# A packed-attention mixer on one core: w1's last quarter, a written plan for batch 0, and the turning of p

## The chip, the core and the metric

The kernel runs on one core of a Trainium2 chip. The metric is the device time of one execution in microseconds. The core's engines are PE (TensorE; its weight loads are shown as PEld), DVE (VectorE), ACT (ScalarE), POOL (GpSimd) and SP (SyncE, which here issues nearly all DMAs). Each engine works through its own list of instructions in order, and waits at an instruction until what it needs is there.

## What is computed

Eight batches, eight heads, 576 tokens, head dimension 64, 32 packing queries per head. Cut to what matters:

```python
def sm_attn(qq, kk, vv):
    s = scale * np.matmul(qq, kk.transpose(0, 1, 3, 2))
    a = np.exp(s - np.max(s, axis=-1, keepdims=True))
    a = a / (np.sum(a, axis=-1, keepdims=True) + 1e-09)
    return np.matmul(a, vv)
p_packed = sm_attn(p, k, v)                  # 32 packed tokens per head
x = sm_attn(q, p_packed, p_packed)           # back to 576 tokens; heads side by side: 512 columns
h = x.transpose(0, 2, 1) @ U @ V             # mixing over tokens, rank 32
u = x + h.transpose(0, 2, 1)
out = u + np.maximum(u @ w_ch1, 0.0) @ w_ch2 # 512 -> 2048 -> 512
```

[...]

## The kernel before

**Products in three parts.** The large products split each operand into a rounded part and a rest (names ending in h and l), and `mm3` (lines 85 to 89) issues three products for one.

**Conversion.** `float32_of` (line 73) makes a 128 x 512 block of 32-bit floats from its bits: one ACT operation (line 79, or line 150 in `test_w1`) and three on DVE (lines 80 to 82). w1 has 16 such blocks, called chunks here, number n holding row block x and column quarter c; chunks 12 to 15 are the last quarter. w2 has 16 row blocks of 128 rows. A w2 row block is also split into w2h and w2l (`split_w2`, line 163): a cast on ACT and a subtraction, on POOL for block 0 and on DVE for the others. Bits land in the tiles `bits` (2 buffers, for the whole kernel) and `bits2` (2 buffers, first stage only). `load_w1` and `load_w2` put the DMAs on SP.

**First stage (lines 513 to 577).** The packing attention runs in 16 units, two per batch (four heads each). For a unit, `a_turn` turns k with PE transposes and copies it out of PSUM as kT, `a_scores` forms scores s_ps from kT and pT, `a_softmax` takes the maximum on DVE (sm) and the exponential on ACT (e), `a_turn_back` transposes it, `a_pack` multiplies by v, `a_heads` turns the result into ppT. Once per batch `a_p` makes pT: it turns p and sets the heads of the second group in swapped pairs. The loop `for i in range(NU)` emits one unit per turn; `turns[i]` says how many w1 chunks are converted in that turn, and the steps of batch 0's own attention (`first`, from `attention(0)`) go three to a turn from turn 4 on. Turn 13 emits `fold(0, 0)`, turn 14 starts w2. In this stage the order of each engine's list isn't the order in which the code stands: a scheduler that estimates times sets it.

**Main stage (from line 579, `manual_schedule`).** Here the engines' lists are in the order of the code. For every batch b and each of 16 steps kt, `gemm1(kt)` computes 128 rows of the hidden layer into h_ps (two banks, tags h0 and h1), which ACT and DVE evict as hh and hl; `gemm2(kt - 1)` multiplies them with the w2 blocks into four accumulators o. `fold(b, c)` multiplies ppT with a quarter of w1 into t_ps and evicts it as wth and wtl, four steps ahead of its use, so `fold(0, 3)`, at kt = 10 of batch 0, is the first to read w1's last quarter. `add_u` adds u at kt = 6. Beside these stand the side steps: the steps of the next batch's attention (`steps`), in batch 0 also the last four pieces of the packing (`rest`) and w2's conversions and splits. Before, an attention step comes after `gemm1` and one at the end of each kt, padded with empty ones; a piece of `rest` or a step is put between the two halves of `gemm2`; a split and a conversion stand at the end of each kt.

Of the kernel before, what the change touches and what calls it, by code (L numbers as in the profile page):

```python
# [20 lines left out]
def packed_attention_mixer_kernel(  # L21
# [27 lines left out]
    nc = tc.nc  # L49
    B, H, S, D = q.shape  # L50
# [4 lines left out]
    P = 128  # L55
# [3 lines left out]
    NK = DF // P  # L59
# [3 lines left out]
    scale = 1.0 / float(D) ** 0.5  # L63
# [7 lines left out]
    U, V, w1, w2 = (a.bitcast(I32) for a in (U, V, w1, w2))  # L71

    def float32_of(x, t, raw, out=None, tested=False):


        low, high = raw[:, :, 0], raw[:, :, 1]
        out = x if out is None else out.bitcast(I32)
        if not tested:
            nc.scalar.activation(t, high.bitcast(F32), AF.Abs, scale=REBIAS)
        nc.vector.tensor_single_scalar(x, t.bitcast(I32), 3, op=ALU.logical_shift_left)  # L80
        nc.vector.scalar_tensor_tensor(x, high, SIGN, x, op0=ALU.bitwise_and, op1=ALU.bitwise_or)  # L81
        nc.vector.scalar_tensor_tensor(out, low, 29, x, op0=ALU.logical_shift_right, op1=ALU.bitwise_or)
        return out.bitcast(F32)
# [7 lines left out]
    const = ctx.enter_context(tc.tile_pool(name="const", bufs=1))  # L91
# [37 lines left out]
    def w2_parts(kt):  # L129
        return tuple(t[:, kt % 4] for t in w2t[kt // 4])  # L130

    def conv_tile(dtype):
        return pipe.tile([P, DM], dtype, name="os", bufs=4)

    def bits_tile():
        return pipe.tile([P, 512, 2], I32, name="bits", bufs=2)

    chunks = [(x, c) for c in range(NPC) for x in range(4)]
# [9 lines left out]
    def test_w1(n):  # L148
        tests[n] = conv_tile(F32)
        nc.scalar.activation(tests[n], bits["w1", n][:, :, 1].bitcast(F32), AF.Abs, scale=REBIAS)  # L150

    def convert_w1(n):
        x, c = chunks[n]
        float32_of(conv_tile(I32), tests.pop(n), bits.pop(("w1", n)), w1t[x][:, QW * c:QW * c + QW], tested=True)

    def load_w2(kt):
        b = bits["w2", kt] = bits_tile()
        nc.sync.dma_start(out=b.rearrange("p x t -> p (x t)"), in_=w2[kt * P:(kt + 1) * P, :])

    def convert_w2(kt):  # L160
        return kt, float32_of(conv_tile(I32), conv_tile(F32), bits.pop(("w2", kt)))

    def split_w2(kt, x):
        hi, lo = w2_parts(kt)
        nc.scalar.copy(hi, x)
        (nc.gpsimd if kt == 0 else nc.vector).tensor_tensor(lo, x, hi.bitcast(F32), op=ALU.subtract)

# [232 lines left out]
    sA = actx.enter_context(tc.tile_pool(name="sA", bufs=2, reuse_waits="tile"))  # L400
# [4 lines left out]
    pn, pT, pps, sums = {}, {}, {}, {}  # L405
# [23 lines left out]
    def a_p(b):  # L429
        t_ps = bank()  # L430
        pT[b] = sA.tile([P, 2, P], F32, name="pT")
        pd = sA.tile([P, 2, 2, D], F32, name="pd", bufs=1)
        nc.gpsimd.tensor_copy(pd, pn[b].unsqueeze(2).to_broadcast([P, 2, 2, D]))
        for i in range(2):
            nc.tensor.transpose(t_ps[:, P * i:P * i + P], pd[:, i].rearrange("p z d -> p (z d)"), ident)
        nc.scalar.activation(pT[b][:, 0], t_ps[:, :P], AF.Copy, scale=scale)
        dst, src = (a.rearrange("p (y z n) -> p z y n", y=2, z=2) for a in (pT[b][:, 1], t_ps[:, P:2 * P]))
        for z in range(2):
            nc.scalar.activation(dst[:, z], src[:, 1 - z], AF.Copy, scale=scale)

    def a_turn(u):
        b, g = UN[u]
# [77 lines left out]
    first = attention(0, res)  # L520
    test_w1(0)

    def some_w1(n):
        convert_w1(n)
        if n + 1 < 16:
            test_w1(n + 1)
        if n + 4 < 16:
            load_w1(n + 4)


    turns = [0, 0] + [1] * 10 + [2, 1, 2, 1]
    n_w1 = 0
    for i in range(NU):
        if i > 0:
            a_turn_back(i - 1, bank_a("m"))
        a_scores(i)
        if i + 1 < NU:
            a_load_v(i + 1)
            a_turn(i + 1)
# [12 lines left out]
        if i >= 4:  # L552
            for _ in range(3):
                if first:
                    first.pop(0)()
        if i == 2:
            uv = load_uv()
        if i == 3:
            prepare_uv(*uv)
        if i == 13:  # L560
            fold(0, 0)
        if i == 14:
            load_w2(0)
            load_w2(1)
            steps = attention(1, res)
            steps.pop(0)()
            split_w2(*convert_w2(0))
            load_w2(2)
# [134 lines left out]
    w2x = None  # L703

    pieces = {3: 2, 8: 0}
    n_w2 = 1

    for n in (20, 19, 18, 15, 15, 14, 13, 12, 12, 11, 5, 0, 0, 0, 0):
        steps.insert(n, lambda: None)
    last, parts = None, []  # L710
    for b in range(B):
        cur = Batch(b)
        oj = None
        ahead = attention(b + 2, res) if b + 2 < B else []
        for kt in range(NK):
            cur.gemm1(kt)
            if b == 0 and kt < 2:
                w2x = convert_w2(n_w2)
                n_w2 += 1
            if oj and kt == 1:  # L720
                store_joint(b - 1, oj)
            if steps and (b < 2 or kt % 4 != 2) and (b, kt) != (1, 0):
                steps.pop(0)()
            if (b, kt) == (0, 5):
                w2_tiles(ctx.enter_context(tc.tile_pool(name="sC", bufs=1, side="right", reuse_waits="tile")), 2)
            if kt > 0:
                cur.gemm2(kt - 1, (rest or steps).pop(0) if b == 0 and (rest or steps) else None)
            elif last:
                last.gemm2(NK - 1)
                last.store()  # L730
                if last.b % 2 == 1:
                    oj = joint(last.b, parts)
            if kt % 4 == 2 and (b, kt) != (B - 1, NK - 2):
                n = b * NPC + kt // 4 + 1
                fold(n // NPC, n % NPC)
            if kt == 6:
                cur.add_u()
            for _ in range(pieces.get(kt, 1)):
                if w2x:
                    split_w2(*w2x)  # L740
                    w2x = None
                    if n_w2 + 1 < NK:
                        load_w2(n_w2 + 1)
                    if 0 < kt and n_w2 < NK:
                        w2x = convert_w2(n_w2)
                        n_w2 += 1
            if steps and kt % 4 != 2 and (b, kt) != (1, 0):
# [45 lines left out]
```

## Time and profile before

| what | us |
|---|---|
| median of 3 runs | 831.68 |
| lowest and highest run | 831.53, 833.7 |
| the profiled execution | 831.53 |
| its span in the profile | 829.7 |
| PE busy in the span | 798.7 |
| DVE, ACT, POOL busy | 351.2, 318.7, 80.1 |

The busy time is a sum over instructions; the overlap of pipelined products is taken out. A row of a timeline has the start in microseconds, the duration, the engine, the line and operation, what it writes and reads, and how many records are grouped; in brackets stands how long the engine had been idle, and what ended that. A row by windows gives, for each stretch, the busy time and number of records of each engine, the clock that PE was granted as a share of the full one, the mean busy share of the DMA engines and their rate in GB/s. A row of waits names the waiting instruction, the instruction it waited for, the sum, the count and the longest. The chain of waits is followed back from the last instruction; its row by line gives the share of the stretch that each line has on it.

### The profile page before, as it was taken

To read this page: it belongs to the slowest core of one execution; us is meant where nothing else is said; L and a number is where in the kernel's file an instruction comes from. 1 tells how busy PE (TensorE), PEld (TensorE's weight loads), DVE (VectorE), ACT (ScalarE), POOL (GpSimd) and SP (SyncE) were. 2 spreads that over 40 slices of the span, in tenths; PEclk is the share of its full clock that TensorE was granted. 3 is DMA by queue.
4 is the path that set the end of the run, shared out by engine and by line. 5 is a ranking of instruction groups with operands and counts; after the bars stand their busy time and mean duration, and the time that the engine had idled before them with its cause. 6 is when DMAs were issued, how large, how long until landed. Compare 5 with 4: busy or idle time off the path is not lost.

```text
span 829.7 us, 15436 instructions
## 1 busy us (share of the span) xinstructions
PE 798.7 (96%) x6224; PEld 643.7 (78%) x6224; DVE 351.2 (42%) x781; ACT 318.7 (38%) x974; POOL 80.1 (10%) x115
## 2 busy tenths in 40 slices
PE   7879698999999999999999999999999999999997
PEld 5556377888788888888888888888888888887886
DVE  3777467773343323433433234333434234332232
ACT  5788664354333332333333232343234232332231
POOL 0222201100111001010011001010101011100000
PEclk8999899999999999999999999999999999999999
DMA  9999764216001220023002120122002200030001
GB/s 299 347 360 358 252 139 127 78 51 188 1 1 47 100 55 2 1 96 92 1 1 89 58 55 2 46 87 57 2 18 90 73 22 1 14 111 1 2 0 64
DMA packets 60310, 70.23 MB, mean 85 GB/s; under 512 B 22864, under 2 KB 41296, under 8 KB 60240
## 3 DMA queue, kind: packets, MB, share of 16 engines
q1 hardware_dynamic: 59920, 68.73, 26.5%
q8 instruction: 49, 0.80, 0.4%
q10 hardware_dynamic: 320, 0.52, 0.2%
q14 instruction: 21, 0.17, 0.1%
HBM read 53.64 MB, written 15.60 MB: 83 GB/s over the span
## 4 chain that ended last, share of the span: by engine, by line
PE 89%; DVE 4%; DMA 3%; ACT 2%; issue 1%; POOL 0%; SPq 0%; ACTq 0%; POOLq 0%
PE o L87 16%; PE o L89 16%; PE o L88 16%; PE h_ps L87 9%; PE h_ps L89 8%; PE h_ps L88 8%; PE t_ps L384 4%; DMA bits<-in_moe_w_ch_dram 2%; PE o L654 2%; PE t_ps L229 2%; DMA vt<-in_v_dram 1%; PE t_ps L327 1%; PE t_ps L249 1%; PE t_ps L255 1%; DVE os L81 1%
## 5 line engine op out<-in xcount | busy, mean ns | idle before, releaser
L87 PE MATMUL o<-w2h,hh 128*128 128x512 f32 x512 | 206.6, 404 | 0.0
L89 PE MATMUL o<-w2h,hl 128*128 128x512 f32 x512 | 202.4, 395 | 0.0
L88 PE MATMUL o<-w2l,hh 128*128 128x512 f32 x512 | 201.9, 394 | 0.0
L637 DVE SCALAR_TENSOR_TENSOR hl<-h_ps,hh 128x256 fp32r<-128x256 f32 x256 | 105.4, 423 | 204.0 <-ACT hj L636 189.9
L634 ACT ACTIVATE hh<-h_ps 128x256 fp32r<-128x256 f32 x256 | 98.6, 386 | 182.9 <-PE h_ps L89 182.5
L87 PE MATMUL h_ps<-ah,wth 128*128 128x320 f32 (+1 forms) x512 | 157.7, 308 | 0.4 <-DVE hl L637 0.3
L88 PE MATMUL h_ps<-al,wth 128*128 128x320 f32 (+1 forms) x512 | 151.6, 296 | 0.0
L89 PE MATMUL h_ps<-ah,wtl 128*128 128x320 f32 (+1 forms) x512 | 151.5, 296 | 0.0
L87 PEld LDWEIGHTS h_ps<-ah,wth 128*128 128x128 f32 x512 | 96.7, 189 | 25.6 <-issue 21.0
L89 PEld LDWEIGHTS o<-w2h,hl 128*128 128x128 f32 x512 | 96.4, 188 | 22.5
L87 PEld LDWEIGHTS o<-w2h,hh 128*128 128x128 f32 x512 | 97.0, 189 | 21.0 <-issue 4.6
L88 PEld LDWEIGHTS o<-w2l,hh 128*128 128x128 f32 x512 | 97.0, 189 | 16.6
L88 PEld LDWEIGHTS h_ps<-al,wth 128*128 128x128 f32 x512 | 96.9, 189 | 1.9
L89 PEld LDWEIGHTS h_ps<-ah,wtl 128*128 128x128 f32 x512 | 97.0, 189 | 0.0
L391 DVE TENSOR_TENSOR wtl<-t_ps,wth 128x256 fp32r<-128x256 f32 x128 | 48.5, 420 | 102.4 <-ACT wth L390 99.0
L390 ACT CAST wth<-t_ps 128x256 fp32r<-128x256 f32 x128 | 43.3, 374 | 110.0 <-PE t_ps L384 102.3
L347 POOL TENSOR_TENSOR al<-aT,ah 128x320 fp32r<-128x320 f32 (+1 forms) x32 | 25.7, 806 | 211.5 <-ACT ah L346 211.5
L290 POOL TENSOR_TENSOR e<-e,m 128x576 f32<-128x576 f32 x16 | 18.6, 1160 | 261.8 <-DVE m L289 261.8
L236 ACT COPY xT<-t_ps 128x256 f32<-128x256 f32 x64 | 21.5, 395 | 38.9 <-PE t_ps L229 38.2
L384 PE MATMUL t_ps<-w1t,ppT 64*32 64x512 f32 x512 | 35.9, 615 | 0.0
L346 ACT CAST ah<-aT 128x320 fp32r<-128x320 f32 (+1 forms) x32 | 13.8, 435 | 43.8 <-DVE aT L345 43.8
L636 ACT ACTIVATE hj<-h_ps 128x64 f32<-128x64 f32 x128 | 28.3, 221 | 0.0
(121 smaller groups left out, 822.3 us busy)
## 6 DMA issues: line engine op xcount, KB each, us to landing
bits<-in_moe_w_ch_dram SPq DMA_DIRECT2D x32, 512.0 KB, 6.4
kx<-in_k_dram SPq DMA_DIRECT2D x16, 576.0 KB, 7.0
x<-in_q_dram SPq DMA_DIRECT2D x16, 576.0 KB, 5.0
vt<-in_v_dram SPq DMA_DIRECT2D x32, 256.0 KB, 6.9
out_dram<-bits SPq DMA_DIRECT2D x32, 256.0 KB, 2.4
aD<-aT SPq DMA_DIRECT2D x16, 288.0 KB, 2.1
aP<-aD SPq DMA_DIRECT2D x32, 128.0 KB, 3.4
ppP<-ppD SPq DMA_DIRECT2D x32, 64.0 KB, 3.1
```

The lines of the kernel that those rows point to most:

```text
L87: nc.tensor.matmul(ps, lhsT=lh, rhs=rh, start=start, stop=False)
L88: nc.tensor.matmul(ps, lhsT=lh, rhs=rl, start=False, stop=False)
L89: nc.tensor.matmul(ps, lhsT=ll, rhs=rh, start=False, stop=stop)
L236: nc.scalar.copy(dst, src[:, a])
L290: nc.gpsimd.tensor_tensor(e, e, m.unsqueeze(2).to_broadcast([P, S // 32, 32]), op=ALU.subtract)
L347: nc.gpsimd.tensor_tensor(al[:, g, ns], aT[:, ns], ah[:, g, ns].bitcast(F32), op=ALU.subtract)
L384: nc.tensor.matmul(f_ps[g][xs], lhsT=ppT[b][zs, g, xs], rhs=w1t[h // 2][zs, QW * c:QW * c + QW], start=True, stop=True)
L390: nc.scalar.copy(hi[:, g], f_ps[g][:, cs])
L391: nc.vector.tensor_tensor(lo[:, g], f_ps[g][:, cs], hi[:, g].bitcast(F32), op=ALU.subtract)
L634: nc.scalar.activation(hh[:, ms], src, AF.Relu)
L636: nc.scalar.activation(hj[:, jslot(self.b, kt), self.js], h_ps[:, LAST], AF.Relu)
L637: nc.vector.scalar_tensor_tensor(hl[:, ms], src, 0.0, hh[:, ms].bitcast(F32), op0=ALU.max, op1=ALU.subtract)
```

## The change

Three things are done. w1's chunks 12 to 15 are no longer converted in the first stage but among batch 0's products, with loads taken in one list (`order`) with w2's. What stands beside batch 0's products is written in a table `plan`: for each kt three places (after `gemm1`, between the halves of `gemm2`, at the end), and letters for a conversion of w2 (c), a split (s), a late w1 chunk (w), an attention step (a) and a piece of `rest` (u). The two tables `turns` and `early` set how many w1 chunks and attention steps each turn of the first stage has. And p is turned without a copy on POOL: four products of p with the identity, or with an identity whose columns are swapped in groups of 32, and one copy out. p's tile pn gets a second buffer, and the split of w2's block 0 is on DVE like the others.

```diff
+    swapped = const.tile([P, P], F32, name="swapped")
+    for z in range(2):
+        a, b = (x.rearrange("p (y z n) -> p z y n", y=2, z=2) for x in (swapped, ident))
+        nc.gpsimd.tensor_copy(a[:, z], b[:, 1 - z])
...
+    plan = (
+        ".cs . .",
+        ".c .u .c",
+        ".a .su .cs",
+        ".a .u .sca",
+        ".a .su .cwa",
+        ". .ca .swa",
...
+    turns = [0, 0, 1, 1, 0, 2, 0, 2, 1, 0, 2, 1, 0, 2, 0, 0]
+    early = [0, 0, 0, 0, 3, 2, 4, 3, 2, 5, 3, 2, 0, 0, 0, 0]
+    NW1 = sum(turns)
...
+    order = list(numbered("c" + "".join(plan)))
+    loads = list(order)
...
-        b = bits["w1", n] = bits_tile() if n % 2 else sA.tile([P, 512, 2], I32, name="bits2")
+        b = bits["w1", n] = bits_tile() if n % 2 or n >= NW1 else sA.tile([P, 512, 2], I32, name="bits2")
...
+    def load_next():
+        if loads:
+            code, n = loads.pop(0)
+            (load_w2 if code == "c" else load_w1)(n)
...
-        (nc.gpsimd if kt == 0 else nc.vector).tensor_tensor(lo, x, hi.bitcast(F32), op=ALU.subtract)
+        nc.vector.tensor_tensor(lo, x, hi.bitcast(F32), op=ALU.subtract)
...
-            pn[b] = sA.tile([P, 2, D], F32, name="pn", bufs=1)
+            pn[b] = sA.tile([P, 2, D], F32, name="pn", bufs=2)
...
-        pd = sA.tile([P, 2, 2, D], F32, name="pd", bufs=1)
-        nc.gpsimd.tensor_copy(pd, pn[b].unsqueeze(2).to_broadcast([P, 2, 2, D]))
-        for i in range(2):
-            nc.tensor.transpose(t_ps[:, P * i:P * i + P], pd[:, i].rearrange("p z d -> p (z d)"), ident)
-        nc.scalar.activation(pT[b][:, 0], t_ps[:, :P], AF.Copy, scale=scale)
-        dst, src = (a.rearrange("p (y z n) -> p z y n", y=2, z=2) for a in (pT[b][:, 1], t_ps[:, P:2 * P]))
-        for z in range(2):
-            nc.scalar.activation(dst[:, z], src[:, 1 - z], AF.Copy, scale=scale)
+        for i, z in product(range(2), range(2)):
+            nc.tensor.matmul(t_ps[D * z:D * z + D, P * i:P * i + P], lhsT=pn[b][:, i], rhs=(ident, swapped)[i],
+                             start=True, stop=True)
+        nc.scalar.activation(pT[b].rearrange("p g n -> p (g n)"), t_ps[:, :2 * P], AF.Copy, scale=scale)
...
-    turns = [0, 0] + [1] * 10 + [2, 1, 2, 1]
...
-        if i >= 4:
-            for _ in range(3):
-                if first:
-                    first.pop(0)()
+        for _ in range(early[i]):
+            first.pop(0)()
...
-    for n in (20, 19, 18, 15, 15, 14, 13, 12, 12, 11, 5, 0, 0, 0, 0):
-        steps.insert(n, lambda: None)
+    def convert():
+        w2x.append(convert_w2(order.pop(0)[1]))
+        load_next()
+
+    def split():
+        split_w2(*w2x.pop(0))
+
+    def convert_late_w1():
+        n = order.pop(0)[1]
+        test_w1(n)
+        convert_w1(n)
+        load_next()
...
+                do(places[0][1:])
...
-                cur.gemm2(kt - 1, (rest or steps).pop(0) if b == 0 and (rest or steps) else None)
+                cur.gemm2(kt - 1, (lambda: do(places[1][1:])) if places else None)
...
-            for _ in range(pieces.get(kt, 1)):
-                if w2x:
-                    split_w2(*w2x)
...
+                do(places[2][1:])
```

What the change moves, at three places. Line numbers in rows of the changed kernel are its own.

POOL, at the end of the first stage, before (ppall is the packed result, w2l the rest of w2's block 0, pd the copy of the last batch's p, al the rest of batch 0's u, e the scores of batch 1):

```order
L347 TENSOR_TENSOR al<-aT_1122,ah 128x256
L493 COPY ppall<-two 128x64
L166 TENSOR_TENSOR w2l_103<-os,w2h_102 128x512
L433 COPY pd<-pn 128x256
L493 COPY ppall<-two 128x64 x4
L290 TENSOR_TENSOR e<-e,m 128x576
```

and now:

```order
L387 TENSOR_TENSOR al<-aT_911,ah 128x320
L387 TENSOR_TENSOR al<-aT_1105,ah 128x320
L529 COPY ppall<-two 128x64
L387 TENSOR_TENSOR al<-aT_911,ah 128x256
L387 TENSOR_TENSOR al<-aT_1105,ah 128x256
L529 COPY ppall<-two 128x64 x5
L330 TENSOR_TENSOR e<-e,m 128x576
```

w2l and pd are gone from POOL, and al stands nearer to the end.

PE, from the last turn of k's before (k_ps) over the last turn of p (t_ps from pd) to unit 14's scores (s_ps), before; m_ps is a turn back or a pack:

```order
L239 MATMUL k_ps<-ident,kx 64x128 x2
L255 MATMUL m_ps<-ident,e_1513 128x128 x4
L257 MATMUL m_ps<-ident,e_1513 64x128
L490 MATMUL m_ps<-vt,eT 32x64 x20
L435 MATMUL t_ps<-ident,pd 128x128 x2
L500 MATMUL t_ps<-ident,two 128x128
L249 MATMUL s_ps<-kT,pT 32x320
```

PE now, from the last turn of p to unit 13's scores:

```order
L279 MATMUL k_ps<-ident,kx 64x128 x2
L473 MATMUL t_ps<-ident,pn 64x128 x2
L473 MATMUL t_ps<-swapped,pn 64x128 x2
L536 MATMUL t_ps<-ident,two 128x128
L295 MATMUL m_ps<-ident,e_1398 128x128 x4
L297 MATMUL m_ps<-ident,e_1398 64x128
L289 MATMUL s_ps<-kT,pT 32x320
```

The last turn of p is read straight from p's own tile and stands a unit earlier. Behind these rows come, now, the fold, a pack, a turn back, unit 14's scores, the turn of unit 15's k, a turn back, unit 15's scores and a pack, and then batch 0's first product; before, the fold came after unit 14's scores, and all turns of k ahead of them.

DVE in batch 0, from the scores of the next batch's first group (e) at kt = 4 to the eviction of kt = 5 (hl), before:

```order
L283 STREAM_TRANSPOSE e_2074<-t_ps_2075 128x320
L284 STREAM_TRANSPOSE e_2074<-t_ps_2076 128x256
L166 TENSOR_TENSOR w2l1_105<-os_2043,w2h1_104 128x512
L80 TENSOR_SCALAR os_2108<-os_2109 128x512
L81 SCALAR_TENSOR_TENSOR os_2108<-bits_2041,os_2108 128x512
L82 SCALAR_TENSOR_TENSOR os_2108<-bits_2041,os_2108 128x512
L289 TENSOR_REDUCE m_2114<-e_2074 128x18
L637 SCALAR_TENSOR_TENSOR hl_2118<-h_ps0_2119,hh_2117 128x256
```

and now:

```order
L323 STREAM_TRANSPOSE e_2021<-t_ps_2022 128x320
L324 STREAM_TRANSPOSE e_2021<-t_ps_2023 128x256
L206 TENSOR_TENSOR w2l1_108<-os_1988,w2h1_107 128x512
L80 TENSOR_SCALAR os_2053<-os_2054 128x512
L81 SCALAR_TENSOR_TENSOR os_2053<-bits_1914,os_2053 128x512
L82 SCALAR_TENSOR_TENSOR os_2053<-bits_1914,os_2053 128x512
L80 TENSOR_SCALAR os_2063<-os_2061 128x512
L81 SCALAR_TENSOR_TENSOR os_2063<-bits_1994,os_2063 128x512
L82 SCALAR_TENSOR_TENSOR w1t0_101<-bits_1994,os_2063 128x512
L329 TENSOR_REDUCE m_2069<-e_2021 128x18
L671 SCALAR_TENSOR_TENSOR hl_2073<-h_ps0_2074,hh_2072 128x256
```

A second conversion, of w1's chunk 12 (w1t0), stands between.

More of the change, by code (lines that the diff above doesn't have):

```diff
@@ L562, in packed_attention_mixer_kernel @@
         if i == 14:
-            load_w2(0)
-            load_w2(1)
+            load_next()
+            load_next()
+            split_w2(*convert_w2(order.pop(0)[1]))
+            load_next()
+        if i == 14:
             steps = attention(1, res)
             steps.pop(0)()
-            split_w2(*convert_w2(0))
-            load_w2(2)
     assert not first
@@ L702, in packed_attention_mixer_kernel, with do @@
     puts.pop()()
-    w2x = None
-    pieces = {3: 2, 8: 0}
-    n_w2 = 1
-    for n in (20, 19, 18, 15, 15, 14, 13, 12, 12, 11, 5, 0, 0, 0, 0):
-        steps.insert(n, lambda: None)
+    w2x = []
+    def convert():
+        w2x.append(convert_w2(order.pop(0)[1]))
+        load_next()
+    def split():
[4 more added lines that the diff above has]
+        convert_w1(n)
+        load_next()
+    codes = {
+        "a": lambda: steps.pop(0)(), "u": lambda: rest.pop(0)(),
+        "c": convert, "s": split, "w": convert_late_w1,
+    }
+    def do(what):
+        for code in what:
+            codes[code]()
     last, parts = None, []
@@ L715, in packed_attention_mixer_kernel @@
         for kt in range(NK):
+            places = plan[kt].split() if b == 0 else None
             cur.gemm1(kt)
-            if b == 0 and kt < 2:
-                w2x = convert_w2(n_w2)
-                n_w2 += 1
             if oj and kt == 1:
                 store_joint(b - 1, oj)
-            if steps and (b < 2 or kt % 4 != 2) and (b, kt) != (1, 0):
+            if places:
+                do(places[0][1:])
+            elif steps and (b < 2 or kt % 4 != 2) and (b, kt) != (1, 0):
                 steps.pop(0)()
@@ L737, in packed_attention_mixer_kernel @@
                 cur.add_u()
-            for _ in range(pieces.get(kt, 1)):
-                if w2x:
-                    split_w2(*w2x)
[L741 to L747, printed above, removed]
+            if places:
+                do(places[2][1:])
+            elif steps and kt % 4 != 2 and (b, kt) != (1, 0):
                 steps.pop(0)()
```

21 lines of the change are left out of this document (19 added, 2 removed).

## The prediction, on record before the changed kernel was timed

> **What bounds the kernel now.** I read the whole span first, then the busy time by stage, then each stage's own waits and chain.
>
> ```profile
> span 829.7 us, 15436 instructions
> ...
> core 0: us, PE busy (x) PEld busy (x) DVE busy (x) ACT busy (x) POOL busy (x), PEclk, DMA share, GB/s
> 31.00:60.00 29.00, 23.65 (x370) 15.70 (x368) 24.32 (x52) 23.87 (x80) 6.45 (x11) 1.00 1.07 353
> 60.00:90.00 30.00, 25.92 (x407) 17.62 (x411) 22.13 (x45) 25.34 (x79) 7.84 (x13) 0.94 1.07 355
> 90.70:103.50 12.80, 6.58 (x100) 3.00 (x99) 6.04 (x13) 5.02 (x17) 1.84 (x3) 0.73 0.61 193
> ...
> 103.50:191.30 87.80, 85.06 (x668) 68.85 (x666) 63.62 (x131) 45.38 (x126) 8.31 (x12) 1.00 0.34 95
> ```
>
> The span is 829.7 us; this execution took 831.53 us (1.8 around the span), 0.15 below the median of 831.68. The sum below is made against 831.53. There are three stages. Up to 90.7 us the packing of p runs with PE, DVE and ACT each about 80 to 86% busy and the DMA engines full: no single bound, but a mesh of short waits. From 90.7 to 103.5 PE works 6.58 of 12.80 us at a granted clock of 0.73. Batch 0 (103.5 to 191.3) has PE busy 85.06 of 87.80 us, so 2.74 us is all that can be won there; later batches are PE throughout and are not touched.
>
> The timeline of the second stage shows the hole:
>
> ```profile
> 89.81 0.90 PE L490 MATMUL m_ps<-vt,eT 128*32 128x64 f32 x40 [0.40 <-ACT eT L471]
> 92.98 0.62 ACT L165 CAST w2h<-os 128x512 fp32r<-128x512 f32 x1 [2.48 <-DVE os L82]
> 93.68 1.26 POOL L166 TENSOR_TENSOR w2l<-os,w2h 128x512 fp32r<-128x512 f32 x1 [4.32 <-ACT w2h L165]
> 94.88 0.40 POOL L433 COPY pd<-pn 128x256 f32<-128x256 f32 x1
> 95.33 0.69 PE L435 MATMUL t_ps<-ident,pd 128*128 128x128 f32 x2 [4.62 <-POOL pd L433]
> 97.24 2.16 PE L384 MATMUL t_ps<-w1t,ppT 64*32 64x512 f32 x16
> 103.53 0.39 PE L87 MATMUL h_ps<-ah,wth 128*128 128x320 f32 x1
> ```
>
> PE ends a pack at 90.71 and waits 4.62 us for pd, the copy of p that its last turn reads. pd needs only p, but stands on POOL behind w2l, which waits for a conversion on DVE and a cast on ACT. Batch 0's first product starts at 103.53.
>
> **The change part by part.**
>
> *The hole: 4.6 us.* pd no longer exists and w2l is on DVE, so the last turn of p waits for p alone. Next late would be kT for the same scores, and PE itself; both are ready by 90.71. Bounds 3.6 (another microsecond wait appears) to 4.62; I take 4.6. The split of w2's row 0 now costs DVE 0.69 (row below) in the first stage, where DVE is not always late: 0 to 0.7, I take 0.2.
>
> *The slow clock behind the hole: 1.7 us.* Two groups that run cold there, in the chain of waits, and the same groups later and earlier:
>
> ```profile
> 96.38 1.40 PE s_ps L249 x8
> 116.80 1.02 PE t_ps L384 x16
> 68.86 0.77 PE s_ps L249 x12
> ```
>
> The fold takes 2.16 us against 1.02, the scores 1.40 against 0.77: 1.77 together. It goes with the hole, unless other gaps bring the clock down: 0 to 1.8, I take 1.7.
>
> *Order of the tail: 0.5 us.* In the second stage PE idles 12.80 - 6.58 = 6.2 us, 1.6 beyond the hole: waits for the softmax of units 14 and 15. Now the turn of unit 15's k and a pack stand in that gap. Bounds -1.6 to 1.6; I take a third.
>
> *Four chunks of w1 leave the first stage: 2.5 us.* The chain of waits over 31 to 90 us and over its second half, by line, and the groups of a conversion:
>
> ```profile
> by line: issue 11.9%; DVE os L81 9.1%; PE k_ps L229 8.6%; DMA vt<-in_v_dram 8.4%; DVE w1t L82 7.9%; PE m_ps L490 7.5%; PE s_ps L249 5.8%; DVE os L80 5.2%; ACT os L150 4.7%; PE m_ps L255 4.5%; ACT kT L236 4.2%; ACT e L462 3.7%; DVE sm L460 2
> by line: issue 15.7%; PE k_ps L229 14.8%; PE m_ps L490 12.0%; PE s_ps L249 11.3%; ACT kT L236 8.2%; PE m_ps L255 7.4%; ACT os L150 7.4%; ACT e L462 7.2%; PE t_ps L327 4.2%; PE t_ps L255 3.4%; PE t_ps L500 2.7%; ACT two L492 2.2%; PE k_ps L2
> ...
> L81 DVE SCALAR_TENSOR_TENSOR os<-bits,os 128x512 int32<-128x512 int32 x13 | 9.1, 703 | 0.2
> L150 ACT ACTIVATE os<-bits 128x512 f32<-128x512 f32 x13 | 9.0, 695 | 1.8 <-DVE os L80 1.8
> L82 DVE SCALAR_TENSOR_TENSOR w1t<-bits,os 128x512 int32<-128x512 int32 x13 | 8.9, 685 | 0.2
> L80 DVE TENSOR_SCALAR os<-os 128x512 int32<-128x512 int32 x13 | 7.2, 555 | 4.1 <-ACT os L150 4.1
> ```
>
> A chunk costs DVE 0.70 + 0.69 + 0.56 = 1.94 us and ACT 0.70. On the chain, 26.9% of 59 us = 15.9 us for 13 chunks, 1.22 each: upper bound 4 x 1.22 = 4.9. The lower bound is 0, where PE takes over at once. In the second half only ACT's 7.4% of 30 us = 2.2 us is left of it and PE leads; so I take half, 2.5. The DMA engines, full at 354 GB/s, do not stand against this: four chunks of 512 KB less are 2.1 MB, 5.9 us. One queue effect: unit 15's k load now stands on SP behind a q load that waits for mix1 to free its tile, and lands late only if it takes longer than the roughly 10 us of PE work between (rows of the order).
>
> ```profile
> kx<-in_k_dram SPq DMA_DIRECT2D x16, 576.0 KB, 7.0
> ```
>
> *p turned by plain products: -1.0 us.* Two transposes become four products with 64 output rows; three ACT copies become one of 256 columns.
>
> ```profile
> 30.71 1.09 PE L229 MATMUL k_ps<-ident,kx 128*128 128x128 f32 x8
> 31.83 1.22 PE L204 MATMUL t_ps<-os,x 128*128 128x144 f32 x8
> 43.30 0.90 PE L490 MATMUL m_ps<-vt,eT 128*32 128x64 f32 x40
> 44.60 0.28 ACT L436 ACTIVATE pT<-t_ps 128x128 f32<-128x128 f32 x1 [0.33 <-PE t_ps L435]
> 44.77 0.34 ACT L439 ACTIVATE pT<-t_ps 128x64 f32<-128x64 f32 x2
> 88.22 0.40 ACT L236 COPY kT<-k_ps 128x256 f32<-128x256 f32 x1
> ```
>
> A transpose takes 1.09 / 8 = 0.136 us. A plain product of 144 columns leaves two records, so 1.22 / 4 = 0.305, or 0.27 for 128 columns: twice a transpose. Four in a row are 1.08 against 0.27: 0.81 per batch, 6.5 us in all. But the pack shows that narrow tiles run side by side: 40 records of 64 columns in 0.90 us are 0.022 each, a third of 0.068. If z = 0 and z = 1 run abreast it is 0.54: 0.27 more per batch, 2.2 us. ACT saves 0.62 - 0.40 = 0.22, 1.8 us in all. On the path between -6.5 and +1.8; nearer the row with tiles abreast, I take -1.0. The Trainium skill, page "TensorE: Matmul & The Clock Gate", section Terms, calls transpose mode four times faster for FP32. By it the four products would cost 2.2 us a batch and the eight batches some 15 us more PE time (an estimate); the row of 144-column products says twice, not four times. The two small copies that make swapped stand where POOL waited for the first load of p, and cost nothing:
>
> ```profile
> 2.83 0.40 POOL L433 COPY pd<-pn 128x256 f32<-128x256 f32 x1 [1.13 <-DMA pn<-in_p_dram]
> ```
>
> *Batch 0: 1.0 us.* It takes over four chunks. PE's waits there, and what DVE and the loads look like:
>
> ```profile
> PE t_ps L249 <- ACT xT L240: 1.8, 1, 1.8
> PE t_ps L500 <- DVE e L283: 0.4, 1, 0.4
> ...
> L166 DVE TENSOR_TENSOR w2l<-os,w2h 128x512 fp32r<-128x512 f32 x15 | 10.3, 689 | 6.2 <-ACT w2h L165 5.7
> ...
> 108.35 0.33 SPq L158 DMA_DIRECT2D bits<-in_moe_w_ch_dram  x1
> 112.69 0.68 ACT L79 ACTIVATE os<-bits 128x512 f32<-128x512 f32 x1
> ...
> 129.31 0.75 DVE L637 SCALAR_TENSOR_TENSOR hl<-h_ps,hh 128x256 fp32r<-128x256 f32 x2
> 134.79 0.74 DVE L637 SCALAR_TENSOR_TENSOR hl<-h_ps,hh 128x256 fp32r<-128x256 f32 x2
> ...
> 107.41 0.40 PE L87 MATMUL o<-w2h,hh 128*128 128x512 f32 x1
> 108.11 0.39 PE L87 MATMUL o<-w2h,hh 128*128 128x512 f32 x1
> ```
>
> The 1.8 us wait is for a turn of q on ACT behind a w2h cast that waited for DVE; the plan puts that turn behind a split whose conversion is one step old, so it should go. Against that DVE gets 4 x 1.94 = 7.8 us: 63.6 + 7.8 = 71.4 of 87.8, so it still has cover. The tightest place is the third piece of order above: a second conversion, 1.94 us, comes into the 5.48 us that lie between two evictions now (129.31 to 134.79). hl is then up to 1.9 us later, but its bank is wanted again only after the twelve products with w2, four times the 0.70 us from 107.41 to 108.11, 2.8 us. Without that cover each such step costs up to 1.9 us, and the plan has five steps with two conversions: -9.5 to +2.7. The cover stands at each of them, so I stay near the upper end, with something left for late evictions: +1.0.
>
> *Sum:* 4.6 - 0.2 + 1.7 + 0.5 + 2.5 - 1.0 + 1.0 = 9.1. 831.5 - 9.1 = 822.4 us.
>
> **The rivals.**
> - *The quarter was not on the path* (the change moves it, but to no gain): PE leads the second half of the first stage, and batch 0 wins nothing. 4.6 - 0.2 + 1.7 - 1.0 = 5.1, so 826.4. For it speaks the chain of 60 to 90 us; against it DVE's share of the first half.
> - *All of it was on the path:* with p at -0.5 and batch 0 at its whole 2.7, 4.6 + 1.8 + 1.6 + 4.9 - 0.5 + 2.7 = 15.1, so 816.4. For it speaks that all three engines get lighter at once, and the DMA with them.
> - *The plain products run one after the other and on the path:* -6.5 in place of -1.0, so 827.9. PE's chain share speaks for it, the pack's tiles abreast against.
> - *Slower: the bits of the added chunks land late.* Two buffers serve 20 conversions instead of 16. Where two conversions stand in one step, the load behind the first is issued about 2.7 us (a conversion and an eviction on DVE) before ACT wants it. If it needs the median of all such loads, 6.4 us, ACT waits 3.7 us with the next eviction of h behind it, and PE waits for that. Four places give 15 us: 822.4 + 1.0 + 15 = 838.4. The kernel is slower than before from 2.0 us a place, a landing time of 4.7 us. Against it: the load of 108.35 was there at 112.69, 4.3 us later, and the DMA share is 0.34.
>
> ```profile
> bits<-in_moe_w_ch_dram SPq DMA_DIRECT2D x32, 512.0 KB, 6.4
> ```
>
> - *The hole only moves:* the new order has another wait of its size in the first stage: 831.
>
> **How the numbers follow.** Forecast 0.50, quarter off the path 0.17, all on it 0.17, products in a row 0.08, late bits 0.05, hole moved 0.03. The range 815 to 828.5 us holds the first four but for their edges. A measurement tells 0.3% (2.5 us) from no change. Faster by more than that means below 829.0: the first four less a few hundredths, 0.88; same 0.07; slower 0.05.
>
> **What would show it.** Right: no wait of PE on POOL before batch 0, the fold at about 1.0 us, a granted clock near 1 in the tail, the first product of batch 0 at about 103.5 - 8.1 = 95.4 us, and no more than 1.7 us of PE waits in batch 0. Wrong: that product at 98 or later (the quarter was off the path), turns of p at 1 us or more, or waits of batch 0's products on hl, xT or the bits above 4 us in all.

## The result, and the profile after

The changed kernel takes 823.39 us (median of 4 runs, 822.64 to 824.23), the kernel before, beside it, 832.69 (4 runs, 831.53 to 834.45). The ratio is 0.9885, with a 95% interval of 0.9867 to 0.9903. The forecast was 822.4 us, with a range of 815 to 828.5. The sum came out; whether its terms did is what the experiments are for. Two single runs of kernels below, 1725.53 us of late_w1_alone and 1969.1 us of three_copies, fell in a slow state and stand in no figure.

The page and the windows of the changed kernel (length, busy time of PE, PEld, DVE, ACT and POOL with the number of records, granted clock, DMA share, GB/s), taken from an execution of 822.64 us:

```profile
span 820.9 us, 15500 instructions
...
0.00:95.49 95.49, 82.84 (x1252) 55.58 (x1253) 58.42 (x123) 69.71 (x214) 15.76 (x35) 0.95 1.00 325
...
84.00:97.00 13.00, 12.31 (x234) 7.98 (x234) 5.72 (x13) 11.20 (x39) 2.11 (x5) 1.00 0.90 279
97.00:185.00 88.00, 87.38 (x672) 70.00 (x672) 73.36 (x145) 47.70 (x130) 8.94 (x12) 1.00 0.46 125
```

And the same stretch of the kernel before, up to its first product of batch 0:

```profile
0.00:103.53 103.53, 80.69 (x1204) 53.83 (x1205) 64.35 (x134) 72.64 (x233) 20.41 (x42) 0.92 0.99 324
```

Ahead of batch 0 PE was busy 80.69 of 103.53 us, so 22.84 idle; now 82.84 of 95.49, 12.65 idle. PE works 2.15 us more there and yet is done 8.04 earlier; 1.08 of the 2.15 lie in its first 24 products, which ran slower in this execution (last section). In the tail (84 to 97, the last 1.5 us of it in batch 0) it is busy 12.31 of 13 us, with a granted clock of 1.00; in the tail before (90.7 to 103.5) it was busy 6.58 of 12.8, with 0.73.

PE's timeline in that tail, p's last turn first:

```profile
84.97 0.44 PE L473 MATMUL t_ps<-ident,pn 128*64 128x128 f32 x4
85.24 0.39 PE L473 MATMUL t_ps<-swapped,pn 128*64 128x128 f32 x4
...
86.86 1.16 PE L424 MATMUL t_ps<-w1t,ppT 64*32 64x512 f32 x16
...
95.49 0.42 PE L87 MATMUL h_ps<-ah,wth 128*128 128x320 f32 x1
```

No bracket stands behind the turn of p: PE did not wait for it. It stands at 84.97, where the kernel before had it at 95.33. Each pair of its products takes 0.27 us from start to start (84.97 to 85.24), so the tiles run abreast: 0.54 a batch, as taken. The fold takes 1.16 us against 2.16. The first product of batch 0 starts at 95.49; 95.4 was forecast. From there to the end of the span it is 725.41 us, against 829.7 - 103.53 = 726.17 before. PE's only wait for another engine in 97 to 185 us:

```profile
PE h_ps L87 <- DVE hl L671: 0.3, 1, 0.3
```

All five marks set for "right" are there. But PE's time up to that product is a sum of many small waits, and the maxima of the units (DVE's reduce, sm) tell that the gain isn't where the term of the quarter put it. Unit 13's maximum, before and now:

```profile
86.38 0.76 DVE L460 TENSOR_REDUCE sm<-s_ps 128x1 f32<-128x576 f32 x1 [1.34 <-PE s_ps L249]
87.27 0.76 DVE L496 TENSOR_REDUCE sm<-s_ps 128x1 f32<-128x576 f32 x1 [2.03 <-PE s_ps L289]
```

Up to there the changed kernel is 0.9 us behind; all of the 8 us come between the scores of unit 13 and the first product. Part of the work has changed sides of that mark, though: the last turn of p now stands ahead of it, the turn of unit 15's k behind it.

### The profile page after: what moved, and what is told of

It reads as the page before. It is cut to its first block, busy times and chain, and to the rows that moved or that the text cites. A ratio compares the mean times of both kernels' runs of the same rounds, so it can differ in the third digit from the quotient of the medians.

```text
span 820.9 us, 15500 instructions
## 1 busy us (share of the span) xinstructions
PE 802.2 (98%) x6272; PEld 645.6 (79%) x6272; DVE 353.9 (43%) x782; ACT 318.4 (39%) x958; POOL 75.5 (9%) x108
## 4 chain that ended last, share of the span: by engine, by line
PE 91%; DMA 4%; ACT 2%; DVE 1%; SPq 1%; issue 1%; POOL 0%; ACTq 0%; POOLq 0%
PE o L87 17%; PE o L89 16%; PE o L88 16%; PE h_ps L87 9%; PE h_ps L88 8%; PE h_ps L89 8%; PE t_ps L424 4%; DMA vt<-in_v_dram 2%; PE o L688 2%; PE t_ps L269 2%; DMA kx<-in_k_dram 2%; PE t_ps L289 1%; PE t_ps L367 1%; PE t_ps L295 1%; PE k_ps L269 1%; DMA bits<-in_moe_w_ch_dram 1%
```

## The experiments

Each kernel was timed against the kernel before (832.55, 832.26 and 832.39 us in the three sets). A kernel has 4 to 11 runs. From its one profile I read the start of batch 0's first product, PE's idle time ahead of it (that start less PE's busy time up to it) and the stretch from it to the end of the span; the profiled execution can lie a microsecond off the median, as in late_split (831.12) and transposes_late (827.08).

| kernel | median us | ratio, 95% interval | first product at | PE idle ahead of it | from there to the end |
|---|---|---|---|---|---|
| before | 832.69 | 1 | 103.53 | 22.84 | 726.17 |
| w2l_alone | 829.67 | 0.9968, 0.9956 to 0.9979 | 101.45 | 20.75 | 726.15 |
| late_split | 830.06 | 0.9971, 0.9961 to 0.9982 | 101.52 | 20.13 | 727.78 |
| p_and_w2l | 828.56 | 0.9953, 0.9938 to 0.9968 | 100.50 | 18.09 | 726.30 |
| w1_early | 827.25 | 0.9936, 0.9924 to 0.9949 | 100.50 | 18.23 | 724.40 |
| late_w1_alone | 827.26 | 0.9927, 0.9913 to 0.9942 | 100.01 | 17.63 | 725.49 |
| transposes_late | 825.97 | 0.9921, 0.9907 to 0.9935 | 99.24 | 15.93 | 726.06 |
| three_copies | 826.38 | 0.9919, 0.9901 to 0.9936 | 100.11 | 17.05 | 725.49 |
| even_early | 825.35 | 0.9919, 0.9903 to 0.9935 | 97.58 | 16.69 | 725.52 |
| even_turns | 824.55 | 0.9908, 0.9892 to 0.9923 | 97.13 | 14.94 | 725.67 |
| six_late | 828.16 | 0.9951, 0.9935 to 0.9966 | 97.26 | 15.46 | 729.64 |
| two_late | 824.13 | 0.9905, 0.9888 to 0.9923 | 96.35 | 12.69 | 725.05 |
| early_spread | 822.85 | 0.9886, 0.9869 to 0.9902 | 96.76 | 12.13 | 724.34 |
| changed kernel | 823.39 | 0.9885, 0.9867 to 0.9903 | 95.49 | 12.65 | 725.41 |

### One part at a time

Three theories at first: A, the hole pays for all; B, the terms as predicted; C, the quarter pays, and in the tail. *p_and_w2l* is the kernel before with the new turn of p and block 0 of w2 (the first 128 rows of w_ch2) split on DVE:

```diff
+            pn[b] = sA.tile([P, 2, D], F32, name="pn", bufs=2)
...
+        for i, z in product(range(2), range(2)):
+            nc.tensor.matmul(t_ps[D * z:D * z + D, P * i:P * i + P], lhsT=pn[b][:, i], rhs=(ident, swapped)[i],
+                             start=True, stop=True)
...
+        nc.vector.tensor_tensor(lo, x, hi.bitcast(F32), op=ALU.subtract)
```

> The kernel before with two parts of the change alone: p turned by plain products (with p's second buffer), and w2's block 0 split on DVE. All 16 chunks of w1 stay in the first stage, batch 0 has its old side steps. Theory A (the hole of 4.6 us behind POOL and its cold clock are what paid; the quarter of w1 paid nothing ahead of unit 13, whose maximum came at 86.4 us before and at 87.3 in the changed kernel): batch 0's first product at 96 to 97 us, 824 to 825 us. Theory B (the terms of the sum as predicted: hole 4.6, clock 1.7, split -0.2, products -1.0): first product at 98.4, 827.5 us. Theory C (the quarter paid in the tail behind unit 13, not ahead of it): first product at 98 to 99, 827 us, with waits of PE for DVE or ACT in the tail.

*w2l_alone* has only the last of these lines:

> The kernel before with one line changed: w2's block 0 is split on DVE. pd then stands on POOL behind nothing that waits for a conversion. Theories A and B: PE's wait for pd falls from 4.6 us to under 0.6, the fold takes about 1.0 us again, 826 to 827 us; against p_and_w2l this gives the price of the plain products: B says 1.0 us faster than that run, A says within 0.5 us of it. If p's copy was itself late (it waits for its load and for a single buffer), the wait stays at 1 us or more and the time is 828 or more.

*late_w1_alone* is the changed kernel with the old turn of p and w2's block 0 split on POOL:

> The changed kernel with p turned as before (copy on POOL, transposes) and w2's block 0 split on POOL again; w1's quarter is late and the plan stands. On POOL w2l now stands ahead of batch 0's al, and pd behind it. Theory A: with fewer conversions in the first stage the split comes early, so the hole is gone here too: PE's wait for pd below 1 us, 823.5 to 825 us. Theory B: the hole is its own part and stays, so 832.7 - 0.5 - 2.5 - 1.0 = 828.7 us, PE waiting 3 us or more for pd.

*w1_early* is the changed kernel with all sixteen chunks in the first stage, in the old places, and the rest of the plan kept:

```diff
-        ".a .su .cwa",
-        ". .ca .swa",
+        ".a .su .ca",
+        ". .ca .sa",
...
-    turns = [0, 0, 1, 1, 0, 2, 0, 2, 1, 0, 2, 1, 0, 2, 0, 0]
+    turns = [0, 0] + [1] * 10 + [2, 1, 2, 1]
```

> The changed kernel with all 16 chunks of w1 converted in the first stage again (the old numbers per turn) and the letters for late chunks taken out of the plan; the rest of the change stands. Theory A: 823.4 to 824.5 us, the first product of batch 0 within 1 us of 95.5. Theory B: 2.5 us later in the first stage, and batch 0 up to 0.5 us shorter: 825.5 to 826.5 us. Theory C: 826, with unit 13's maximum at 87.3 as in the changed kernel and the loss behind it.

p and w2l together are worth 4.0 us, not the 8 of theory A, which falls; none of the three theories met 828.56. w1_early is slower than all three had it, and its unit 13 comes at 90.10, not at 87.3, so C falls too. The step from w1_early to the changed kernel (the quarter and the new turns) is worth 3.9, more than B had for it. late_w1_alone, 827.26, lies between A and B, but A's mechanism is there: w2l runs early on POOL, and PE turns the last p without a wait for it.

```profile
80.42 1.27 POOL L202 TENSOR_TENSOR w2l<-os,w2h 128x512 fp32r<-128x512 f32 x1 [6.18 <-ACT w2h L201]
93.36 0.44 PE L471 MATMUL t_ps<-ident,pd 128*128 128x128 f32 x2
```

So each half of the change takes the hole away by itself. What became of it is seen in w2l_alone, whose timeline has, on PE and on ACT:

```profile
91.64 0.44 PE L435 MATMUL t_ps<-ident,pd 128*128 128x128 f32 x2
93.98 0.62 ACT L165 CAST w2h<-os 128x512 fp32r<-128x512 f32 x1 [2.48 <-DVE os L82]
94.50 0.27 ACT L436 ACTIVATE pT<-t_ps 128x128 f32<-128x128 f32 x1
94.83 0.83 PE L249 MATMUL s_ps<-kT,pT 64*32 64x320 f32 x16 [2.65 <-ACT pT L436]
95.29 2.07 PE L384 MATMUL t_ps<-w1t,ppT 64*32 64x512 f32 x16
```

The wait for POOL is gone and p is turned at 91.64. But its copy pT stands on ACT behind w2h, which waits 2.48 us for the conversion on DVE: the same chain that held pd on POOL now holds pT on ACT, and PE waits 2.65 us one step later. The fold behind that wait still takes 2.07 us, so little of the slow clock's term is won.

### Taking the second wait away too

*late_split* puts the whole split of block 0 behind batch 0's first products:

```diff
-            split_w2(*convert_w2(0))
+            first_w2 = convert_w2(0)
...
             cur.gemm1(kt)
+            if (b, kt) == (0, 0):
+                split_w2(*first_w2)
```

> The kernel before with w2's block 0 split on DVE (as in w2l_alone, 829.67) and the whole split, cast and subtraction, put behind the first products of batch 0. In w2l_alone pT's copy stands on ACT behind the cast w2h, which waits 2.48 for the conversion on DVE, and PE then waits 2.65 for pT. Theory L, that wait is what was left of the hole: it goes, with up to 0.5 of slow clock, first product of batch 0 at 98.3 to 99.0 in place of 101.45, 826.5 to 827.3. Theory M, another wait of its size is next late: first product at 100.5 or later, 829.0 to 829.7.

830.06: theory M by the first product, 101.52, though the time lies 0.4 above its range. The wait for pT is down to 0.26 us, and nothing is won. POOL's copy of the last p, PE's timeline, and the first microseconds of batch 0 (a row by windows):

```profile
92.04 0.53 POOL L433 COPY pd<-pn 128x256 f32<-128x256 f32 x1 [1.19 <-DMA pn<-in_p_dram]
92.62 0.44 PE L435 MATMUL t_ps<-ident,pd 128*128 128x128 f32 x2 [0.41 <-POOL pd L433]
93.43 0.77 PE L249 MATMUL s_ps<-kT,pT 64*32 64x320 f32 x16 [0.26 <-ACT pT L436]
96.88 0.66 PE L255 MATMUL m_ps<-ident,e 128*128 128x128 f32 x4 [1.82 <-ACT e L462]
97.57 0.76 PE L249 MATMUL s_ps<-kT,pT 64*32 64x320 f32 x16
100.01 1.45 PE L490 MATMUL m_ps<-vt,eT 128*32 128x64 f32 x40 [0.83 <-ACT eT L471]
101.52 0.61 PE L87 MATMUL h_ps<-ah,wth 128*128 128x320 f32 x1
101.50:104.00 2.50, 2.50 (x11) 2.50 (x12) 0.00 (x0) 1.08 (x4) 0.24 (x1) 0.50 0.05 13
```

Behind p's last turn come the last two units in series: scores, maximum, exponential, transposes, pack. With nothing left to put between, PE waits at each link (1.82, 0.83), and the last pack takes 1.45 us instead of 0.90. The hole was not a delay in front of work that was ready; it stood ahead of a chain that takes 9 us from p's turn (92.62) to the first product (101.52) even without it. Against w2l_alone the chain is 0.9 us shorter (there 91.64 to 101.45), but p's turn comes 1.0 later: pd now waits for the load of p itself. And behind those waits batch 0 starts at a granted clock of 0.50, with a first product of 0.61 us against 0.39 in the kernel before; that is where most of its 727.78 us against 726.15 comes from. This execution is one of the longer of the eleven (828.87 to 831.59), but even the shortest is above theory L's 827.3.

### p's turn in the changed kernel

*transposes_late* takes the old turn back into the changed kernel, with w2l on DVE (so that pd does not stand behind it).

> The changed kernel with p turned as before: a copy on POOL (pd), two transposes, three copies on ACT, one buffer of pn; w2's block 0 is split on DVE and four chunks of w1 are late as in the changed kernel, which took 823.39. Prediction's term (plain products cost 1.0): 822.4. Theory G, the plain products gain what they gained with all chunks early (p_and_w2l 828.56 against w2l_alone 829.67, 1.1): 824.5, first product of batch 0 at 96.5. Theory H, the parts need each other, so that without the products little is left over late_w1_alone (827.28): 826 to 827, first product at 98.5 to 100.

825.97, theory H: the plain products, priced at a loss of 1.0, are a gain of 2.6 here. With one buffer of pn the load of the last p is issued at 82.28 us (63.96 in the changed kernel), POOL copies it behind al, and PE turns it late:

```profile
82.28 0.55 SPq L451 DMA_DIRECT2D pn<-in_p_dram  x1
87.55 1.42 POOL L383 TENSOR_TENSOR al<-aT,ah 128x256 fp32r<-128x256 f32 x2 [2.15 <-ACT ah L382]
88.91 0.40 POOL L469 COPY pd<-pn 128x256 f32<-128x256 f32 x1
92.44 0.44 PE L471 MATMUL t_ps<-ident,pd 128*128 128x128 f32 x2
```

That is 7.5 us behind the changed kernel's turn (84.97). The row has no bracket: PE didn't stand idle for pd, the turn has a late place in PE's list. *three_copies* keeps the plain products and takes the three copies on ACT back:

```diff
-            nc.tensor.matmul(t_ps[D * z:D * z + D, P * i:P * i + P], lhsT=pn[b][:, i], rhs=(ident, swapped)[i],
+            nc.tensor.matmul(t_ps[D * z:D * z + D, P * i:P * i + P], lhsT=pn[b][:, i], rhs=ident,
...
-        nc.scalar.activation(pT[b].rearrange("p g n -> p (g n)"), t_ps[:, :2 * P], AF.Copy, scale=scale)
+        nc.scalar.activation(pT[b][:, 0], t_ps[:, :P], AF.Copy, scale=scale)
+        dst, src = (a.rearrange("p (y z n) -> p z y n", y=2, z=2) for a in (pT[b][:, 1], t_ps[:, P:2 * P]))
+        for z in range(2):
+            nc.scalar.activation(dst[:, z], src[:, 1 - z], AF.Copy, scale=scale)
```

> The changed kernel (823.39) with p's four plain products all against the plain identity, and three copies on ACT that swap the heads, in place of one copy. Theory I, the plain products gain by ACT's copies (0.62 against 0.40 us for each of 8 batches, 1.8): 825.2, first product of batch 0 at 97.2. Theory J, they gain because the turn no longer hangs on POOL's copy and on one buffer of pn (in transposes_late the last p is loaded at 82.3 and copied at 88.9, behind al): 823.4 to 824.0, first product at 95.5 to 96.2.

With 826.38 it is slower than either theory had it, and no faster than transposes_late (825.97); its five runs spread from 823.71 to 827.36, and the interval of the ratio (0.9901 to 0.9936) just touches the changed kernel's. The profile, of its longest run, speaks against J:

```profile
87.73 0.66 PE L473 MATMUL t_ps<-ident,pn 128*64 128x128 f32 x8
```

The last p is turned 4.7 us ahead of transposes_late (92.44), without POOL and with two buffers, and yet the first product comes at 100.11, not ahead of 99.24 there. So an early turn alone brought nothing in this run. Whether the 2.6 us hang on the time of ACT's copies or on the order that the scheduler makes with them stays open.

### The quarter, or the places?

*even_turns* keeps the quarter late but spreads the twelve early chunks as before:

```diff
-    turns = [0, 0, 1, 1, 0, 2, 0, 2, 1, 0, 2, 1, 0, 2, 0, 0]
+    turns = [0, 0] + [1] * 10 + [1, 0, 1, 0]
```

> The changed kernel with its twelve early chunks spread as before, one behind each of units 2 to 11 and one behind 12 and 14, in place of 0, 0, 1, 1, 0, 2, 0, 2, 1, 0, 2, 1, 0, 2, 0, 0. Theory D, what counts is that four conversions leave ACT and DVE ahead of PE's exponentials (w1_early to the changed kernel: 3.9 for four, 1.0 a chunk): 823.4 to 824.0, first product of batch 0 at 95.5 to 96. Theory E, what counts is behind which unit a conversion stands (two fall behind unit 12 and 14 here, none behind 14 in the changed kernel): 825.5 to 827, first product at 97.5 to 99.

*two_late* keeps chunks 12 and 13 in the first stage, behind unit 14 (turns ends in 0, 2, 2, 0):

> The changed kernel with only chunks 14 and 15 late; 12 and 13 stand behind unit 14. Theory D (1.0 a chunk): 825.3, first product of batch 0 at 97.5 to 98. Theory E (a conversion behind unit 14 stands ahead of the last scores and costs as all four do): 826.5 to 827.3, first product at 99.5 to 100.5. If the tail has room for them: 823.4.

*six_late* moves chunks 10 and 11 out too (turns ends in 0, 0, 0, 0; two more w in the plan, at kt 2 and 3):

> The changed kernel with six chunks of w1 late in place of four: chunks 10 and 11 are converted behind blocks 2 and 3 of the first batch, and the two behind unit 13 leave the first stage. Theory D (1.0 a chunk, wherever it stood): 821.4, first product of batch 0 at 93.5, and from the first product to the end 725.4 as in the changed kernel. Theory E (only conversions in the tail count, and two leave it): 821.4 too, but by units behind 13 alone. Theory F, batch 0 has no cover left for more (ACT waited there for bits up to 2.9 in one wait): first product at 93.5 to 95.5 and 727 to 729 from there, 822.5 to 824.5.

*early_spread* moves none, but spreads all sixteen like the changed kernel:

```diff
-    turns = [0, 0] + [1] * 10 + [2, 1, 2, 1]
+    turns = [0, 0, 1, 1, 1, 2, 1, 2, 1, 1, 2, 1, 1, 2, 0, 0]
```

> All sixteen chunks of w1 in the first stage, as in w1_early (827.25), but none behind units 14 and 15: the changed kernel's table of turns, with one chunk more at units 4, 6, 9 and 12. Theory D, what counts is that conversions leave the stage: 826.3 to 827.3, first product of batch 0 at 99.5 to 100.5. Theory E, what counts is that none stands behind the last units: 823.8 to 825.0, first product at 96.5 to 98.0.

Theory D (1.0 us for each chunk that leaves) falls. early_spread, with the same work as w1_early, is 4.4 us faster (the intervals are far apart) and equal to the changed kernel: the quarter need not leave at all. six_late says the same from the other side: two chunks more have left, and its first product comes at 97.26, where D had 93.5 and the changed kernel has 95.49. even_turns, 824.55, lies between D and E. Theory E in its sharp form, none behind the last units, falls as well: two_late has two behind unit 14 and takes 824.13. What is left is the order as a whole. One place where it differs can be followed. In w1_early, DVE, POOL and PE around unit 10:

```profile
68.47 1.16 POOL L341 TENSOR_TENSOR e<-e,s 128x576 f32<-128x576 f32 x1 [0.16 <-DVE s L340]
68.63 1.55 DVE L82 SCALAR_TENSOR_TENSOR w1t<-bits,os 128x512 int32<-128x512 int32 x1
70.17 0.73 DVE L496 TENSOR_REDUCE sm<-s_ps 128x1 f32<-128x576 f32 x1
71.82 0.66 PE L295 MATMUL m_ps<-ident,e 128*128 128x128 f32 x4 [1.64 <-ACT e L498]
72.41 1.31 PE L289 MATMUL s_ps<-kT,pT 64*32 64x320 f32 x16
73.65 1.54 PE L295 MATMUL t_ps<-ident,aT 128*128 128x128 f32 x6
...
82.73 0.68 DVE L82 SCALAR_TENSOR_TENSOR w1t<-bits,os 128x512 int32<-128x512 int32 x1
83.87 0.44 PE L473 MATMUL t_ps<-ident,pn 128*64 128x128 f32 x4 [1.13 <-DVE aT L385]
```

The same in early_spread:

```profile
68.61 0.64 DVE L82 SCALAR_TENSOR_TENSOR w1t<-bits,os 128x512 int32<-128x512 int32 x1
69.56 0.75 DVE L496 TENSOR_REDUCE sm<-s_ps 128x1 f32<-128x576 f32 x1
71.13 0.87 PE L295 MATMUL t_ps<-ident,aT 128*128 128x128 f32 x6 [0.74 <-DVE aT L345]
71.84 0.60 PE L295 MATMUL m_ps<-ident,e 128*128 128x128 f32 x4
72.37 0.76 PE L289 MATMUL s_ps<-kT,pT 64*32 64x320 f32 x16
```

In w1_early the end of a conversion stands ahead of unit 10's maximum, PE waits 1.64 us for the exponential, and what follows runs slow (scores 1.31 against 0.76, transposes 1.54 against 0.87). In early_spread PE has other transposes to do first. Unit 12's maximum comes at 86.59 in w1_early and at 83.76 in early_spread, though w1_early was 1.1 us ahead at unit 11. A second such place lies between: at 82.73 the end of a conversion stands ahead of DVE's aT, and PE waits 1.13 us for it. That these places make the whole 4.4 us isn't shown.

*even_early* leaves all work alone and only spreads the steps of batch 0's attention evenly:

```diff
-    early = [0, 0, 0, 0, 3, 2, 4, 3, 2, 5, 3, 2, 0, 0, 0, 0]
+    early = [0, 0, 0, 0] + [3] * 8 + [0] * 4
```

> The changed kernel with the steps of batch 0's attention three to a turn from turn 4 to 11, as before, in place of 3, 2, 4, 3, 2, 5, 3, 2. Nothing is more or less work; the scheduler orders the first stage anew. If such a new order is worth little: 823.0 to 824.0, first product of batch 0 at 95.0 to 96.2. If the table carries a part of the gain, or the order by itself moves the stage by a microsecond or two: 824.5 to 825.5, first product at 96.7 to 97.7.

825.35, 2.0 us slower by the medians, with intervals that meet at 0.9903. Its tail has a wait that the changed kernel lacks:

```profile
95.13 0.65 PE L295 MATMUL m_ps<-ident,e 128*128 128x128 f32 x4 [1.10 <-ACT e L498]
```

So a new order of the same work moves the time by 2 to 4 us, as much as most of the terms of the sum.

### How much batch 0 takes

The last column of the table is the price in batch 0. The plan alone brings it from 726.2 to 724.4; two late chunks cost 0.7, four 1.0 to 1.7, six 5.3. In six_late two loads of bits came late:

```profile
119.56 0.67 ACT L185 ACTIVATE os<-bits 128x512 f32<-128x512 f32 x1 [2.08 <-DMA bits<-in_moe_w_ch_dram]
121.81 0.66 ACT L79 ACTIVATE os<-bits 128x512 f32<-128x512 f32 x1 [1.59 <-DMA bits<-in_moe_w_ch_dram]
122.38 0.35 ACT L280 COPY xT<-t_ps 64x256 f32<-64x256 f32 x1
122.78 0.77 PE L289 MATMUL t_ps<-xT,ppT 64*32 64x320 f32 x16 [2.44 <-ACT xT L280]
```

ACT waits 3.7 us for bits with xT queued behind, and PE waits 2.44 for xT: the mechanism of the rival "bits land late". In the changed kernel ACT waits for bits too (up to 2.9 us at once), but PE's products cover it.

## Why the prediction came out, point by point

The forecast of 9.1 us met 9.3 (832.69 to 823.39; 9.2 against the 832.55 of the first set of experiments), and the forecast of the first product 8.1 met 8.04. That the sum came out so well is luck: terms that were wrong in opposite ways made it so.

- **The hole, w2l and the slow clock: 4.6 - 0.2 + 1.7 = 6.1, measured 2.9** (w2l_alone). The step that failed is "Next late would be kT for the same scores, and PE itself; both are ready by 90.71". pT was next late, behind w2h on ACT; and with that gone too (late_split, 2.3) p's own load was (pd waits 1.19 us for it), and then the serial chain of units 14 and 15. The slow clock stayed with the wait (a fold of 2.07 us). The rival "the hole only moves" had half of the truth. With the term of p the forecast for this half of the change is 5.1; p_and_w2l measured 4.0.
- **p by plain products: -1.0, measured +1.1 from w2l_alone to p_and_w2l (intervals overlap) and +2.6 in the changed kernel.** PE's part was right: the tiles run abreast, 0.54 us a batch. The step that failed is that this time was put on the path as a loss. The turn also came free of POOL and of pn's one buffer and stands 7.5 us earlier; that this is the gain isn't shown, and three_copies, with the early turn and no gain, speaks against it as the only cause. What the gain hangs on stays open.
- **Order of the tail and the quarter: 0.5 + 2.5 = 3.0, measured 4.4 (9.2 by the medians, less 2.9, 1.1 and batch 0's 0.8), and not for the reason given.** The step that failed is reading a conversion's share of the chain (1.22 us a chunk, of which half) as what its removal brings. The four chunks bring nothing that the new places don't (early_spread 822.85): its first product is 1.3 us behind the changed kernel's (96.76 against 95.49, two single executions), and batch 0 gives that back (724.34 against 725.41). The rival "the quarter was not on the path" was right in its mechanism and wrong in its time, 826.4, because it gave the tables of turns no worth of their own.
- **Batch 0: +1.0, measured +0.8** (726.17 to 725.41). Its halves hold as well: the 1.8 us wait for xT goes with the plan (w1_early 1.8 less), four late chunks cost 1.0 (724.40 to 725.41). That batch 0 had cover was right, but it ended when chunks 10 and 11 were put at kt 2 and 3 as well.

By the medians the two halves of the change add up: p with w2l 4.0, the rest (late_w1_alone) 5.3, together 9.3 against 9.2. Inside the halves the price of a part depends on what stands beside it: p is worth 1.1 in the kernel before and 2.6 in the changed one, w2l 2.9 there and 1.3 here (827.26 to 825.97, intervals that overlap). So a term of the sum has no price of its own in this stage.

## What to carry to other kernels

Price a hole by what stands behind it, not by its length: follow the work after it to the next barrier, and see whether anything is left to lie beside that chain. Where a scheduler sets the order, run one kernel that moves the work without removing it before you credit a gain to the removal; here equal work in other places was worth 4.4 us. And ask of an engine that feeds the critical one not how busy it is but what stands ahead of the one operation that is waited for.

## What the runs showed of the hardware

**PE's pace at the start varies.** The same 24 products at the start took from 4.30 to 5.49 us over the fourteen profiles; before and after:

```profile
1.06 4.30 PE L513 MATMUL t_ps<-os 128*128 128x128 f32 x24 [1.06 <-DVE os L510]
```

```profile
1.06 5.38 PE L549 MATMUL t_ps<-os 128*128 128x128 f32 x24 [1.06 <-DVE os L546]
```

Windows of 1 us show a step in the pace, in the kernel before at 4 us:

```profile
3.00:4.00 1.00, 1.00 (x7) 1.00 (x7) 0.00 (x0) 0.00 (x0) 0.22 (x1) 1.00 0.65 205
4.00:5.00 1.00, 1.00 (x11) 1.00 (x11) 0.00 (x0) 0.00 (x0) 0.00 (x0) 1.00 1.03 396
```

and in the changed kernel no step up to 6 us, where the 24 are nearly through:

```profile
4.00:5.00 1.00, 1.00 (x6) 1.00 (x6) 0.00 (x0) 0.00 (x0) 0.00 (x0) 1.00 1.04 401
5.00:6.00 1.00, 1.00 (x7) 1.00 (x6) 0.00 (x0) 0.00 (x0) 0.00 (x0) 1.00 1.03 396
```

PE goes from 7 records a microsecond to 11, and the granted clock reads 1.00 in all four rows. The Trainium skill, page "TensorE: Matmul & The Clock Gate", section Part 1, says that PE starts at half clock, and that the window that releases it runs free of the kernel's start. The trace agrees by its pace, not by its column of the clock. The start of a single profile therefore varies by about 1 us that no change made; the later start of the changed kernel's first unit (maximum at 10.57 against 9.10) is mostly of that kind. It needn't reach on: w2l_alone starts with 5.49 us and has its first maximum at 10.28, but its sixth at 38.86, against 39.08 in the kernel before.

**A wait of 1.64 us was followed by slower products** (the scores of 1.31 us above, against 0.76), with a granted clock of 0.83 over 70 to 80 us of w1_early. The Trainium skill, same page and section, speaks of an idle window of about 3.4 us. Here a shorter wait went before, in a stretch of transposes and narrow tiles; which of them counted isn't shown.

**DVE is held up beside POOL.** The last step of a conversion takes 0.69 us, and 1.55 where POOL's e had begun before it (68.47 to 69.63 us in w1_early above). In early_spread DVE begins first, at 68.61, and takes 0.64; there POOL's e takes 1.49 us instead of 1.16:

```profile
68.78 1.49 POOL L341 TENSOR_TENSOR e<-e,s 128x576 f32<-128x576 f32 x1 [0.16 <-DVE s L340]
```

The Trainium skill, page "GPSIMD Engine Reference", section Specifications, says that POOL shares its access to SBUF with DVE and contends with DVE's instructions of two SBUF inputs. This one reads bits and os, and the trace agrees.
